# Threshold attention and gated MLP: first pair shaped in the score banks, and another order of the PSUM banks in the tail

## Chip, cores and metric

The kernel runs on one core of a Trainium2 chip. The metric is the device time of one execution in microseconds (us); the time of a version is the median over its runs.

## What is computed

Eight batches, eight heads, 576 positions, 64 channels a head. The attention keeps only the scores that lie within tau = 0.02 of the largest of their row; its output is the input of a gated MLP with 512 inputs and 1024 inner channels.

```python
scores = scale * np.matmul(q, k.transpose(0, 1, 3, 2))           # scale = 1/8
thresh = np.max(scores, axis=-1, keepdims=True) - tau
scores = np.where(scores >= thresh, scores, -1000000000.0)
attn = softmax(scores);  x = matmul(attn, v), heads side by side  # (8, 576, 512)
h = np.maximum(x @ w_in, 0.0);  u, v = h[..., :512], h[..., 512:]
v_n = (v - mean(v)) / sqrt(var(v) + 1e-6)
v_s = einsum('ts,bsd->btd', w_spatial, v_n) + b_spatial[None, :, None]
out = (u * v_s) @ w_out
```

## The kernel before

**Units of work.** Two heads form a pair; there are 32 pairs, four a batch. A pair has five chunks of query rows: four of 128 (c = 0 to 3), and a rest of 64 rows; the rests of two neighbouring pairs are joined into one chunk of 128 rows (c = 4), done with the odd pair. That makes 144 steps. The order is written out by hand: each engine does its instructions in program order, and only semaphore waits decide when.

**Before a pair's scores** q and k must be transposed, so that channels lie on partitions. `shape_qk` (L130) copies a pair's loaded q and k into transposable form on GpSimd (POOL); for the first pair `shape_first` (L142) does it on VectorE (DVE), ScalarE (ACT) and POOL at once. Then come three jobs on TensorE (PE): `qk_main(i, 0)` transposes the four blocks of q and ACT copies them, times 1/8, into `qkT` (L243, L248); `qk_main(i, 1)` does so for k (L243, L250); `qk_rem` transposes the one block that holds the last 64 rows of q and of k (L259), ACT copies it into `qkT` (L262), and from there the last 64 keys are copied into `kd`, a block-diagonal matrix of both heads, by two copies of 64x64 (L267): DVE for the first pair, POOL for all others. In the head of the program these three jobs of pair 0 stand alone, one after the other (L773), after 14 dummy transposes (L769) that keep PE busy.

**A step** (`step`, L558) first issues the scores on PE: one matmul a pair against `kd` for the 128 last keys of both heads (L529), and one a head for the first 512 keys (L534). Then come one or two other jobs on PE (transposes of the next pair, probabilities times values, MLP matmuls), the row maximum on DVE (L570), the exponentials on ACT (L593, or L587 and L589 for chunks 2 and 4), and the thresholding of the step before on DVE (L551), after which SyncE (SP) issues the transposing DMA of the probabilities, `pT` (L555; L546 for joined chunks, into `ptr`). Two steps or more later `pv` and `pv_rest` multiply by the values (L273, L278), and DVE divides by the row sums (L285, L287). The MLP of a batch runs 26 steps and more after the batch began, as jobs in the steps: `moe_v` (L402, L387, L390), `moe_u` (L444, L449), `moe_s` (L474, L479) and `moe_o` (L503).

**PSUM** has eight banks of 512 floats a partition. In the steps six belong to the pool `ps_s`: two score tiles `s` of three banks each, in turn. The other two are the pool `ps_f` (tiles `f`, one bank each, in turn), for every other job. A tile of a pool waits until all that read the tile before it in the same place are done[...].

**The tail** begins when step 143, the last, is issued. The pool `ps_s` is closed and its six banks become single-bank tiles `t` of a pool `ps_t`; each waits for the score tile that lay there. Jobs that are still due then follow each other without score steps (`run`, L806): `moe_v(6, 4)`, `pv_rest(15)`, `moe_u(6, 1)`, `moe_o(5, 0)`, `x_pe(30)` (L351), `moe_u(6, 2)`, `moe_o(5, 1)`, `moe_u(6, 3)`, `pv(31, 0)`, `moe_o(5, 2)`, `moe_u(6, 4)`, `moe_o(5, 3)`, `pv(31, 1)`, the `moe_s(6, ...)`, and then the last batch (`last_gmlp`, L618). `bank` (L220) chooses the place: its counter runs from the start of the program, and every fourth tile is an `f`, the others are `t`. In the profiled execution the first twelve places of the tail are, by the names in the trace, t t t f t t t f t t t f.

Of the kernel before, what the change touches and what calls it, by code (L numbers as in the profile page):

```python
# [8 lines left out]
F32 = mybir.dt.float32  # L9
# [8 lines left out]
def kernel(  # L18
# [17 lines left out]
    nc = tc.nc  # L36
    B, H, S, D = q.shape
    assert (B, H, S, D) == (8, 8, 576, 64)
    scale = 0.125
# [3 lines left out]
    P = 128  # L43
    const = ctx.enter_context(tc.tile_pool(name="const", bufs=1))
    qkn = ctx.enter_context(tc.tile_pool(name="qkn", bufs=2))
    qkT = ctx.enter_context(tc.tile_pool(name="qkT", bufs=2))
# [12 lines left out]
    ps_s = inner.enter_context(tc.tile_pool(name="ps_s", bufs=2, space=PSUM))  # L59

    identf = const.tile([P, P], F32, name="identf")
# [13 lines left out]
    kd_ring = [const.tile([P, P], F32, name=f"kd{i}") for i in range(2)]  # L75
# [25 lines left out]
    def load(i, n, w, eng=nc.sync):  # L101

        b, hp = divmod(i, HP)
        t = ld_ring[i // 2 % 2][w][:, 2 * (i % 2):2 * (i % 2) + 2 * n]
        src = (q, k, v)[w][b, 2 * hp:2 * hp + 2 * n]

        def main():
            eng.dma_start(
                out=t[:, :, 0:4, :],
                in_=src[:, 0:512, :].rearrange("h (p c) d -> p h (c d)", c=4))  # L110

        def rest():

            u = ld_ring[i // 2 % 2][(0, 0, 2)[w]][(slice(0, 64), slice(64, 128), slice(0, 64))[w]]
            eng.dma_start(out=u[:, 2 * (i % 2):2 * (i % 2) + 2 * n, 4, :],
                          in_=src[:, 512:576, :].rearrange("h p d -> p h d"))

        def rest_b():
            nc.sync.dma_start(
                out=vx_ring[i // 2 % 2][64:128],  # L120
                in_=src.rearrange("(j h) s d -> h s j d", h=2)[1, 512:576])
        return [main, rest] + ([rest_b] if w == 2 else [])
# [5 lines left out]
    nat = {}  # L128
# [39 lines left out]
    def load_w_in(f):  # L168
        nc.sync.dma_start(out=wsl[f % 3].rearrange("p c s -> p (c s)")[:, 0:1024],
                          in_=moe_w_in[f * P:(f + 1) * P, :])  # L170
# [46 lines left out]
    wide = []  # L217
    turn = [0]

    def bank(dtype=F32, n=512):  # L220
        turn[0] += 1
        if wide and turn[0] % 4:
            return wide[0].tile([P, n], dtype, name="t")
        return ps_f.tile([P, n], dtype, name="f")

    def bank16():

        return bank(BF16, 640)

    qks, pts, xns, xts = {}, {}, {}, {}  # L230
# [4 lines left out]
    def qk_main(i, which):  # L235
        hold = {}

        def mm():
            if which == 0:
                qks[i] = qkT.tile([P, 2, S], F32, name="qkT")  # L240
            t = hold["t"] = bank()
            for c in range(4):
                nc.tensor.transpose(out=t[:, c * P:(c + 1) * P], in_=nat[i][which][:, c, :],  # L243
                                    identity=identf)

        def ev():
            if which == 0:
                nc.scalar.mul(out=qks[i][:, 0, 0:512], in_=hold["t"], mul=scale)  # L248
            else:
                (nc.scalar.copy if i else nc.vector.tensor_copy)(out=qks[i][:, 1, 0:512],  # L250
                                                                 in_=hold["t"])
        return "act", mm, ev

    def qk_rem(i):
        hold = {}

        def mm():
            t = hold["t"] = bank()
            nc.tensor.transpose(out=t[:, 0:P], in_=nat[i][0][:, 4, :], identity=identf)  # L259

        def ev():
            nc.scalar.copy(out=qks[i][:, :, 512:576],  # L262
                           in_=hold["t"][:, 0:P].rearrange("p (w s) -> p w s", w=2))
            kd = kd_ring[i % 2]
            for lo in (0, 64):
                hs = slice(lo, lo + 64)
                (nc.gpsimd if i else nc.vector).tensor_copy(out=kd[hs, hs],  # L267
                                                            in_=qks[i][hs, 1, 512:576])
        return "act", mm, ev

    def weigh(t, at, pt, vt):

        nc.tensor.matmul(out=t[:, at:at + 130], lhsT=pt[:, 4, :],  # L273
                         rhs=vt[:, 4:6, :].rearrange("p b d -> p (b d)"),
                         start=True, stop=False)
        for h in range(2):
            for j in range(4):
                nc.tensor.matmul(out=t[:, at + 65 * h:at + 65 * h + 65], lhsT=pt[:, 5 * h + j, :],  # L278
                                 rhs=vt[:, 6 * h + j, :], start=False, stop=(h == 1 and j == 3))
# [454 lines left out]
    for b in range(B):  # L734
        n = dict.fromkeys("vuso", 0)
        for j, t in enumerate(ORDER):
            f = {"v": moe_v, "u": moe_u, "s": moe_s, "o": moe_o}[t]
# [14 lines left out]
    with tc.manual_schedule():  # L752
        for w in (0, 1):
            for f in load(0, 1, w, (nc.sync, nc.scalar)[w]):
                f()
        make_identity(nc, identf)
        clear()
        nc.vector.memset(ntau, -float(tau))
        nc.vector.memset(mhalf, -0.5)
        nc.scalar.activation(out=ctau, in_=ntau, func=ACT.Exp)  # L760
        nc.vector.tensor_copy(out=identb, in_=identf)
        for w in (0, 1):
            for f in load(1, 1, w):
                f()
        for f in load(0, 2, 2):
            f()
        for j in range(3):
            load_w_in(j)
        for _ in range(14):  # L769
            nc.tensor.transpose(out=ps_f.tile([P, 512], F32, name="f")[:, 0:P], in_=identf,  # L770
                                identity=identf)
        shape_first()
        for f in (qk_main(0, 0), qk_main(0, 1), qk_rem(0)):  # L773
            f[1]()
            f[2]()
        shape_qk(1)
        queue = []
        for g, (i, c) in enumerate(steps):
            if c == 2 and i + 2 < NPAIR:
                shape_qk(i + 2)  # L780
            if c == 0:
                shape_v(i)
            if c == 0 and i % 2 and i + 3 < NPAIR or g == 0:
                for w in range(3):
                    queue.extend(load(i + (3 if g else 2), 2, w))
            if g in chores:
                chores[g][0](chores[g][1])
            fs, small_ones = [], []
            if i + 1 < NPAIR and c < 3:
                fs.append(qk_rem(i + 1) if c == 1 else qk_main(i + 1, c // 2))  # L790
            if i and c == (2 if i % 2 else 3):
                fs.append(pv(i - 1, 0))
            if i > 1 and c == 4:
                fs.append(pv(i - 2, 1))
            if i % 2 and c == 3:
                fs.append(pv(i - 1, 1))
            if i % 2 and i > 1 and c == 1:
                small_ones = [pv_rest(i // 2 - 1)]
                fs += small_ones
            fs += [f(*a) for f, *a in jobs.get(g, [])]  # L800
            fs.sort(key=lambda f: (f[0] == "dve", f in small_ones))
            sends += queue[:1 if g > 3 else 2]
            del queue[:1 if g > 3 else 2]
            step(i, c, fs)

        def run(*fs):  # L806
            for f in fs:
                f[1]()
                f[2]()
                for f in sends:  # L810
                    f()
                sends.clear()
        while held:
            held.pop(0)()
        mask()
        inner.close()
        wide.append(ctx.enter_context(tc.tile_pool(name="ps_t", bufs=6, space=PSUM,
                                                  reuse_waits="tile")))
        for _, f in later:
            f()  # L820
        last = [f(b, j) for f, b, j in last]
        run(last[0], pv_rest(NPAIR // 2 - 1), *last[1:3], x_pe(NPAIR - 2), *last[3:6],
            pv(NPAIR - 1, 0), *last[6:], pv(NPAIR - 1, 1), moe_s(Z - 1, 0), moe_s(Z - 1, 1),
            x_pe(NPAIR - 1, True), *[moe_s(Z - 1, j) for j in range(2, 5)])
        rest = last_gmlp(Z)
        next(rest)
        run(moe_u(Z, 0), moe_u(Z, 1))
        next(rest)
        run(*[moe_u(Z, j) for j in range(2, 5)], *[moe_o(Z - 1, j) for j in range(4)])
        next(rest)  # L830
        next(rest, None)
# [35 lines left out]
```

## Time and profile before

| | us |
|---|---|
| median of 6 runs | 483.67 |
| lowest and highest run | 481.24, 485.29 |
| profiled execution, its own time | 482.22 |
| its span, first to last instruction | 480.4 |
| PE busy in the span | 449.0 (93%) |
| DVE busy | 416.7 (87%) |
| ACT busy | 381.8 (79%) |
| POOL busy | 226.6 (47%) |
| first score matmul starts | 8.52 |
| last step's row maximum, start and end | 438.03, 439.39 |
| last step's exponentials, start and end | 439.41, 440.79 |

In a view's line the first numbers are start and duration in us from the start of the span, then engine, source line, operation, output and inputs, with the number of instructions merged into the line; brackets hold the idle time before it and what ended it. PEld is the weight load of a matmul. The chain of waits goes back from the last instruction to what released each one. A table of stretches gives busy time and instruction count of each engine, then the granted clock of PE as a part of full speed (PEclk), the busy share of the 16 DMA engines and GB/s.

### The profile page before, as it was taken

To read this page: it belongs to the slowest core of one execution; us is meant where nothing else is said; L and a number is where in the kernel's file an instruction comes from. 1 tells how busy PE (TensorE), PEld (TensorE's weight loads), DVE (VectorE), ACT (ScalarE), POOL (GpSimd) and SP (SyncE) were. 2 spreads that over 40 slices of the span, in tenths; PEclk is the share of its full clock that TensorE was granted. 3 is DMA by queue.
4 is the path that set the end of the run, shared out by engine and by line. 5 is a ranking of instruction groups with operands and counts; after the bars stand their busy time and mean duration, and the time that the engine had idled before them with its cause. 6 is when DMAs were issued, how large, how long until landed. Compare 5 with 4: busy or idle time off the path is not lost.

```text
span 480.4 us, 9896 instructions
## 1 busy us (share of the span) xinstructions
PE 449.0 (93%) x3664; PEld 238.3 (50%) x3664; DVE 416.7 (87%) x563; ACT 381.8 (79%) x665; POOL 226.6 (47%) x403
## 2 busy tenths in 40 slices
PE   7788788889999999999999999999999999997995
PEld 4344444444554555554555545555554545444542
DVE  4899999989989997999889989899889988897573
ACT  2788787998879798788979898789978888896251
POOL 3462435784438543474417642475337733352021
PEclk8999999999999999999999999999999999999999
DMA  7799999979999799898979889997997999765423
GB/s 236 198 206 213 211 229 193 233 167 191 182 198 196 169 218 209 196 168 190 214 174 223 184 201 212 199 172 174 212 209 189 182 170 206 161 114 111 133 82 117
DMA packets 231120, 89.38 MB, mean 186 GB/s; under 512 B 200608, under 2 KB 225312, under 8 KB 231072
## 3 DMA queue, kind: packets, MB, share of 16 engines
q1 hardware_dynamic: 230416, 87.86, 85.8%
q8 instruction: 29, 0.48, 0.4%
q0 software_dynamic: 160, 0.52, 0.3%
q10 hardware_dynamic: 496, 0.36, 0.2%
q14 instruction: 19, 0.16, 0.1%
HBM read 33.31 MB, written 9.44 MB: 89 GB/s over the span
## 4 chain that ended last, share of the span: by engine, by line
PE 47%; DVE 22%; ACT 21%; issue 5%; DMA 3%; POOL 0%; SPq 0%; POOLq 0%; ACTq 0%; DVEq 0%
PE s L534 13%; DVE negm L570 10%; DVE p L551 8%; ACT e L593 5%; PE f L243 5%; PE f L503 4%; ACT e L587 4%; PE f L278 4%; PE s L529 4%; DMA pT<-p 3%; PE f L444 3%; ACT vrel L412 2%; ACT sq L426 2%; ACT p L589 2%; PE f L273 2%
## 5 line engine op out<-in xcount | busy, mean ns | idle before, releaser
L570 DVE TENSOR_REDUCE negm<-s 128x2 f32<-128x1152 f32 x144 | 194.8, 1353 | 27.5 <-PE s L534 27.0
L534 PE MATMUL s<-qkT 64*128 64x512 f32 (+1 forms) x640 | 162.9, 639 | 0.0
L551 DVE SCALAR_TENSOR_TENSOR p<-e,ctau 128x1152 bf16<-128x1152 f32 x96 | 138.7, 1445 | 1.4 <-ACT e L593 1.2
L593 ACT ACTIVATE e<-s,negm 128x576 f32<-128x576 f32 x192 | 131.8, 742 | 6.5 <-DVE negm L570 6.2
L587 ACT ACTIVATE e<-s,negm 128x576 f32<-128x576 f32 x96 | 65.9, 738 | 19.7 <-DVE negm L574 11.1
L529 PE MATMUL s<-kd,qkT 128*128 128x128 f32 (+1 forms) x320 | 64.7, 305 | 14.2 <-ACT e L593 9.6
L267 POOL COPY kd<-qkT 64x64 f32<-64x64 f32 x62 | 30.4, 491 | 93.9 <-ACT qkT L262 92.1
L529 PEld LDWEIGHTS s<-kd,qkT 128*128 128x128 f32 (+1 forms) x320 | 44.4, 180 | 33.8 <-ACT e L593 19.7
L534 PEld LDWEIGHTS s<-qkT 64*128 64x128 f32 (+1 forms) x640 | 42.1, 175 | 18.3 <-issue 3.0
L420 POOL TENSOR_SCALAR nmean<-sm 128x1 f32<-128x1 f32 (+1 forms) x35 | 15.2, 435 | 69.7 <-ACT vrel L412 64.4
L278 PEld LDWEIGHTS <-pT 128*128 128x128 bf16 x1024 | 41.8, 97 | 7.3 <-issue 4.8
L278 PE MATMUL f<-v,pT 128*128 128x65 bf16 x992 | 44.9, 194 | 0.0
L136 POOL COPY qn<-ql 128x640 f32<-128x640 f32 x31 | 34.8, 1122 | 21.1 <-DMA ql<-in_k_dram 16.2
L589 ACT ACTIVATE p<-e 128x1152 bf16<-128x1152 f32 x32 | 37.2, 1164 | 1.0
L250 ACT COPY qkT<-f 128x512 f32<-128x512 f32 x31 | 18.2, 587 | 16.8 <-PE f L243 16.8
L273 PE MATMUL f<-v,pT 128*128 128x130 bf16 x124 | 27.2, 220 | 3.7 <-ACT qkT L250 1.6
L432 POOL TENSOR_SCALAR vn<-vrel,rs,nm 128x512 bf16<-128x512 f32 (+1 forms) x34 | 28.5, 840 | 3.7
L474 PE MATMUL f<-wsT,vn 128*128 128x512 bf16 x120 | 29.8, 379 | 0.0
L402 PE MATMUL f<-w_in,xT 128*128 128x512 bf16 x112 | 28.9, 380 | 0.0
L444 PE MATMUL f<-xT,w_in 128*128 128x512 bf16 x108 | 27.9, 380 | 0.8 <-DVE xn L287 0.8
L287 DVE TENSOR_TENSOR xn<-f,r 128x256 bf16<-128x256 f32 x62 | 26.3, 425 | 2.1
L248 ACT ACTIVATE qkT<-f 128x512 f32<-128x512 f32 x32 | 18.8, 589 | 10.7 <-PE f L243 10.0
(163 smaller groups left out, 639.6 us busy)
## 6 DMA issues: line engine op xcount, KB each, us to landing
vl<-in_v_dram SPq DMA_DIRECT2D x16, 512.0 KB, 4.7
ql<-in_q_dram SPq DMA_DIRECT2D x15, 512.0 KB, 4.8
kl<-in_k_dram SPq DMA_DIRECT2D x15, 512.0 KB, 4.7
out_dram<-o SPq DMA_DIRECT2D x20, 256.0 KB, 3.2
uT<-in_moe_w_in_dram SPq DMA_DIRECT2D x3, 512.0 KB, 5.4
uT<-in_moe_w_spatial_dram SPq DMA_DIRECT2D x2, 576.0 KB, 4.5
vl<-in_v_dram SPq DMA_DIRECT2D x16, 64.0 KB, 4.4
pT<-p SPq DMA_TRANSPOSE x64, 5.6
```

The costliest lines, as they stand in the source:

```text
L136: nc.gpsimd.tensor_copy(out=t, in_=ld_ring[i // 2 % 2][w][:, 2 * (i % 2):2 * (i % 2) + 2].rearrange("p h c d -> p c h d"))
L267: (nc.gpsimd if i else nc.vector).tensor_copy(out=kd[hs, hs], in_=qks[i][hs, 1, 512:576])
L273: nc.tensor.matmul(out=t[:, at:at + 130], lhsT=pt[:, 4, :], rhs=vt[:, 4:6, :].rearrange("p b d -> p (b d)"), start=True, stop=False)
L278: nc.tensor.matmul(out=t[:, at + 65 * h:at + 65 * h + 65], lhsT=pt[:, 5 * h + j, :], rhs=vt[:, 6 * h + j, :], start=False, stop=(h == 1 an ...
L444: nc.tensor.matmul(out=t, lhsT=w_in[:, m, f * P:(f + 1) * P], rhs=xts[b][:, m, 0:512], start=(m == 0), stop=(m == 3))
L529: nc.tensor.matmul(out=view(s[rows], 512, [[448, 2], [1, 64]]), lhsT=qks[n][:, 0, m], rhs=kd_ring[n % 2], start=True, stop=True)
L534: nc.tensor.matmul(out=s[rows, 1024 * h:1024 * h + 512], lhsT=qks[n][hs, 0, m], rhs=qks[n][hs, 1, 0:512], start=True, stop=True)
L551: nc.vector.scalar_tensor_tensor(out=pt[:, c % 2, :], in0=ef, scalar=ctau, in1=ef, op0=ALU.is_ge, op1=ALU.mult)
L570: nc.vector.tensor_reduce(out=nm, in_=s, axis=AX.X, op=ALU.max, negate=True)
L587: nc.scalar.activation(out=e[:, h, :], in_=s[:, h, :], func=ACT.Prelu, bias=nm[:, h:h + 1], scale=by, alpha=1e30)
L589: nc.scalar.activation(out=pr_ring[i // 2 % 2] if c == 4 else p_ring[2 * (i % 2) + c // 2][:, c % 2], in_=e.rearrange("p h s -> p (h s)"), ...
L593: nc.scalar.activation(out=e[:, h, :], in_=s[:, h, :], func=ACT.Exp, bias=nm[:, h:h + 1])
```

## The change

Three things. Pair 0 gets a function of its own, `first`, in place of `qk_main(0, 0)`, `qk_main(0, 1)` and `qk_rem(0)`: nine transposes, five of q into one score tile and four of k into another, without a wait for banks between them; then ACT copies q, two DVE copies fill `kd` straight from PSUM, ACT and DVE copy one half of k each, and ACT copies the last block. `qk_main` and `qk_rem` lose their branches for pair 0; for the other pairs they are what they were. And `bank` counts from the start of the tail alone and gives in every eight tiles the places t f f t t t t t.

```diff
     def bank(dtype=F32, n=512):
-        turn[0] += 1
-        if wide and turn[0] % 4:
-            return wide[0].tile([P, n], dtype, name="t")
+        if wide:
+
+            turn[0] += 1
+            if turn[0] % 8 not in (2, 3):
+                return wide[0].tile([P, n], dtype, name="t")
         return ps_f.tile([P, n], dtype, name="f")
...
+    def first():
+
+        qkt = qks[0] = qkT.tile([P, 2, S], F32, name="qkT")
+        ts = [ps_s.tile([P, 1536], F32, name="s") for _ in range(2)]
+        for t, w, c, at in ([(ts[0], 0, c, c * P) for c in range(5)]
+                            + [(ts[1], 1, c, c * P) for c in range(4)]):
+            nc.tensor.transpose(out=t[:, at:at + P], in_=nat[0][w][:, c, :], identity=identf)
+        nc.scalar.mul(out=qkt[:, 0, 0:512], in_=ts[0][:, 0:512], mul=scale)
+        for lo in (0, 64):
+            hs = slice(lo, lo + 64)
+            nc.vector.tensor_copy(out=kd_ring[0][hs, hs], in_=ts[0][hs, 576:640])
+        nc.scalar.copy(out=qkt[:, 1, 0:256], in_=ts[1][:, 0:256])
+        nc.vector.tensor_copy(out=qkt[:, 1, 256:512], in_=ts[1][:, 256:512])
+        nc.scalar.copy(out=qkt[:, :, 512:576],
+                       in_=ts[0][:, 512:640].rearrange("p (w s) -> p w s", w=2))
...
         shape_first()
-        for f in (qk_main(0, 0), qk_main(0, 1), qk_rem(0)):
-            f[1]()
-            f[2]()
+        first()
         shape_qk(1)
```

## The prediction

> **What bounds the kernel now.** I first read the page's busy shares and chain: no engine is full, and the end is set by PE, DVE and ACT in turn.
>
> ```profile
> PE 449.0 (93%) x3664; PEld 238.3 (50%) x3664; DVE 416.7 (87%) x563; ACT 381.8 (79%) x665; POOL 226.6 (47%) x403
> PE 47%; DVE 22%; ACT 21%; issue 5%; DMA 3%; POOL 0%; SPq 0%; POOLq 0%; ACTq 0%; DVEq 0%
> ```
>
> So the 144 steps drive themselves: a step starts when the last ends, and loads are issued from the steps. Time gained before the first step should arrive at the last, if nothing tied to the clock on the wall lies between. The change touches only the two ends, so I read those closely. The chain of waits, 6 to 11 us:
>
> ```profile
> 6.21 0.61 ACT qkT L248
> ...
> 6.95 0.32 PE f L259
> ...
> 7.29 0.28 ACT qkT L262
> ...
> 7.59 0.19 DVE kd L267
> ...
> 7.79 0.69 DVE kd L267
> ...
> 8.52 0.49 PE s L529 x2
> 9.01 1.57 PE s L534 x4
> ```
>
> From the q copy to the first scores each step waits for the one before: L259 for the bank that q leaves, then a copy, then `kd` from that copy. Then the table of stretches, cut where PE's clock changes:
>
> ```profile
> 5.98:9.39 3.41, 1.80 (x11) 1.13 (x11) 1.55 (x3) 0.86 (x2) 1.28 (x2) 1.00 0.95 246
> 9.39:12.81 3.42, 3.42 (x12) 1.75 (x10) 1.36 (x1) 1.15 (x3) 0.90 (x2) 0.51 0.96 369
> 16.22:19.63 3.41, 1.87 (x10) 0.80 (x10) 3.38 (x5) 2.31 (x5) 0.83 (x1) 1.00 0.29 72
> ```
>
> After 3.41 us in which PE was busy for only 1.80, the next 3.42 run at half clock, with PE busy throughout. Last, the timeline where the tail starts:
>
> ```profile
> 438.03 1.35 DVE L570 TENSOR_REDUCE negm<-s 128x2 f32<-128x1152 f32 x1
> 438.49 0.58 ACT L459 ACTIVATE uT<-f 128x512 bf16<-128x512 f32 x1
> 439.41 1.37 ACT L593 ACTIVATE e<-s,negm 128x576 f32<-128x576 f32 x2 [0.34 <-DVE negm L570]
> 439.49 0.10 PEld L273 LDWEIGHTS <-ptr 128*128 128x128 bf16 x1 [0.83 <-issue]
> 439.50 0.42 DVE L287 TENSOR_TENSOR xn<-f,r 128x256 bf16<-128x256 f32 x1
> 440.84 0.22 PE L273 MATMUL t<-v,ptr 128*128 128x130 bf16 x1 [1.69 <-ACT e L593]
> 442.31 1.03 PE L503 MATMUL f<-w_o,gT 128*128 128x512 bf16 x4
> ```
>
> The first `t` (`moe_v(6, 4)`, 438.09) waits for nothing late, but the second, `pv_rest`, starts only when the last step's exponentials end. So it lies where the last score tile was. Meanwhile the `f` banks fall free at 439.07 (L459 ends) and 439.92 (L287 ends), unused until 442.31. From 440.84 to 473.32 the chain is PE alone, without a gap: what PE gains here, the end gains.
>
> [...] here one 53% busy was followed by the dip, while 1.87 us (55%) from 16.22 was not. [...] in `x_pe(31)` both read halves of one bank, and DVE starts as ACT ends:
>
> ```profile
> 452.06 0.37 ACT L360 COPY xT<-f 128x256 bf16<-128x256 bf16 x1 [3.52 <-PE f L354]
> 452.46 0.29 DVE L361 COPY xT<-f 128x256 bf16<-128x256 bf16 x1
> ```
>
> [...]
>
> **The head, step by step.** Transposes: q's four finish as before (6.19). The fifth needs POOL's L149, which ended at 5.80; it costs one slot. Four k transposes' loads take 0.59 us, so 0.15 a slot: the fifth is done about 6.35, k's four at 6.61 + 0.15 = 6.76, plus 0.04 for the wait. ACT: q 6.21 to 6.82 as before; half of k, 0.37 (L360's row is bf16 but has 256 columns; the 64x256 float copy L695 took 0.37 too): to 7.19; last block, 0.27 as L262: to 7.46. DVE: two `kd` copies from PSUM of 64 columns. No such row exists: between 0.17 (L285, 4 columns from PSUM) and 0.42 (L491, 256 columns)[...]. I take 0.2 each, 6.37 to 6.8, ends 6.7 and 7.2; either way ahead of ACT. DVE's half of k shares its bank with ACT's, so it follows at 7.22 and takes 0.42: to 7.64. The first score tile takes the place of the first transposes' tile, so L529 waits for all its readers, the last being ACT at 7.46; L534 wants DVE's half of k at 7.68, but L529 before it lasts to 7.99. **First score 7.5 for 8.52: 1.0 us.** Bounds: 0.6 (slow `kd` copies and ACT's last copy queued behind them) to 1.2.
>
> The clock. With PE at work 5.98 to 6.8 and from 7.5 on, the window to 9.39 is 2.7 us busy of 3.41, well over the 1.80. Even if the dip came all the same, at the same place, more of PE's work lies before it: L534 at full clock takes 1.1 instead of 1.57 (7.99 to 9.1), the transposes L243 0.6 instead of 1.04 (qn was ready at 8.42), to 9.7; L529 and L534 of the second step at half clock 1.92 as now, to 11.6 instead of 13.54. The row maximum of step 1 ends at 13.0, thresholding of step 0 (1.42, free to start as its exponentials end about 12.0) at 14.4, and the third row maximum starts at 14.4, where the chain has it at 16.38. **So 2.0 us by then, 1.0 of it the clock's.** Without a dip it is about 2.5. [...]
>
> What could stop it on the way: POOL's copy of pair 2 waits for its load until 18.80, wherever the steps are; PE wants it at 23.37, now 21.4, and it ends at 19.7. The first transposing DMA (issued 19.19) would come at 17.2; the loads ahead of it leave the DMA engines idle from 17.2 to past 20, so it has room. Every later DMA is issued from steps. SP and POOL get no added instruction; two copies stay on DVE.
>
> **The tail.** `pv_rest` goes to the first `f`: start 439.13 (439.07 and a wait) for 440.84, takes 0.61; `moe_u(6, 1)` to the second: 439.98 (behind it PE's queue waits, as now), 0.86, to 440.84; `moe_o(5, 0)` to the second `t`, free at 440.84: where it now starts at 442.31. **1.47 us.** Behind it all banks are free or reused after eight tiles, as now. One guard: the last `pT`, issued at 442.3 and 4.6 us on its way, lands at 446.9; `pv(31, 1)` is due at 448.80 − 1.47 = 447.3, its weights 0.2 earlier. Margin 0.2, so I take **1.4**. ACT can't follow at first (440.68 on), but the banks give it four tiles of slack.
>
> ```profile
> L555 SPq DMA_TRANSPOSE pT<-p x2: 2683/2708/2733, 438.2 to 442.3; - x2
> ...
> DMA to landing us min/median/max: 4.6/4.6/4.6
> ```
>
> Bank copies of pairs 1 to 31 are untouched: 0.
>
> **Sum.** 2.0 + 1.4 = 3.4 on the profiled execution's 482.22 (span 480.4 and 1.8 around it): 478.8. That execution is 1.45 below the median of the runs, 483.67; off the median it is 480.3, or 481.3 for runs without a dip. I say 480.5.
>
> **Rivals.** *Only the tail counts* (14%): the head's gain is lost among steps that wait for transposing DMAs (3% of the chain). For: DMA engines are over 90% busy in many slices. Against: they are idle before the first transpose. 483.67 − 1.4 = 482.3. *Only the head counts* (13%): the last `pT` lands later, as the median of 5.6 us over all would have it: 447.9, 0.8 behind its weights' due time, and what hangs on it keeps PE waiting; then some 0.6 of the tail is left at best, none if more is late: 481.1 to 481.7. *Slower* (6%): the shift moves `pT` behind 512 KB loads more often. The chain holds two such waits, 6.47 and 7.18 us, against 4.7 for the shortest at the start: some 2.3 each. From the second more on the gain is gone; with three more, 480.5 + 6.9 = 487.4. Against: all are issued from the same queue in the same order. *It doesn't do what it says* (3%): were the `f` banks not free first, or the tiles' waits wider, 483.7.
>
> **Numbers.** The forecast case has 64%, its own range 479.0 to 481.9. A measurement tells 0.5% (2.4 us) from no change at best, so faster means under 481.25: four fifths of the forecast case and part of the second rival. The range 478.8 to 483.0 leaves out the slower case, part of "nothing happens", and gains over the bound.
>
> **What would show it.** First L529 near 7.5; no `f` tile in the head but the dummies; DVE's half of k right after ACT's; PEclk at 1.00 through 9.4 to 12.8, or L534 of step 0 at 1.1; the first `pT` issued about 17; in the tail `pv_rest` on an `f`, 0.4 to 0.5 us after `moe_v(6, 4)`'s last matmul instead of 2, and `moe_o(5, 0)` right as the last exponentials end, then PE without gaps. I'm wrong if PE stalls at `pv(31, 1)`, or the last exponentials end less than 1 us earlier than 440.79.

## Result, and the profile after

The changed kernel takes 479.78 us (median of 29 runs, 478.32 to 482.92), the kernel before 482.75 beside it (64 runs, 480.13 to 487.45): a ratio of 0.9946, interval 0.9932 to 0.9959. By that ratio it is 2.6 us less; the two medians by themselves are 3.0 apart. The profiled executions are 478.95 and 482.22 us, 3.3 apart. In the fences of after, line numbers are higher by 16 from `pv` on (L529, L534, L570 and L551 of before are L545, L550, L586 and L567); `first` is L277 to L284.

The page's busy shares and the chain's shares by engine:

```profile
PE 447.4 (94%) x3664; PEld 237.8 (50%) x3664; DVE 416.5 (87%) x563; ACT 381.6 (80%) x666; POOL 225.7 (47%) x403
PE 46%; DVE 24%; ACT 21%; issue 6%; DMA 2%; POOL 1%; POOLq 0%; ACTq 0%; DVEq 0%
```

The work is the same and so is its mix; only the two ends moved. The chain of waits of after, from the transposes to the third row maximum:

```profile
5.24 1.08 PE s L277 x5
6.34 0.61 ACT qkT L278
6.97 0.22 DVE kd L281
7.20 0.24 DVE kd L281
7.46 0.28 ACT qkT L284
7.78 0.49 PE s L545 x2
...
13.93 1.28 DVE negm L586
```

The first score starts at 7.78 (8.52 before) and the third row maximum at 13.93 (16.38). The steps between are handed on one by one: q's copy starts only when the fifth transpose, in the next bank of the same tile, has ended; the `kd` copies, which read that other bank, start only when q's copy has ended. The timeline shows DVE idle until ACT's copy of q is done:

```profile
6.97 0.46 DVE L281 COPY kd<-s 64x64 f32<-64x64 f32 x2 [2.42 <-ACT qkT L278]
6.99 0.37 ACT L282 COPY qkT<-s 128x256 f32<-128x256 f32 x1
```

So these readers of one score tile take turns, though they read different banks of it. (DVE's half of k starts at 7.46, when DVE is done with `kd`; whether it also waited for ACT can't be seen here.) The table of stretches at the same times as before (columns: stretch, its length, busy us of PE, PEld, DVE, ACT, POOL, then PE's clock, the DMA share, GB/s):

```profile
5.98:9.39 3.41, 2.58 (x13) 1.47 (x12) 0.89 (x4) 1.23 (x3) 1.27 (x2) 1.00 0.83 233
9.39:12.81 3.42, 2.68 (x15) 1.49 (x17) 2.91 (x3) 2.30 (x5) 1.30 (x4) 1.00 0.85 302
16.22:19.63 3.41, 1.65 (x13) 0.59 (x14) 3.01 (x3) 3.12 (x4) 0.22 (x1) 1.00 1.01 222
```

PE has 2.58 us of work where it had 1.80, and the stretch behind it, at 0.51 before, runs at 1.00. Last the tail's timeline:

```profile
437.26 0.22 PE L289 MATMUL f<-v,ptr 128*128 128x130 bf16 x1
437.56 1.37 ACT L609 ACTIVATE e<-s,negm 128x576 f32<-128x576 f32 x2 [0.34 <-DVE negm L586]
438.13 1.04 PE L460 MATMUL f<-xT,w_in 128*128 128x512 bf16 x4
439.00 1.03 PE L519 MATMUL t<-w_o,gT 128*128 128x512 bf16 x4
```

`pv_rest` now stands ahead of the last exponentials, on an `f`; `moe_u(6, 1)` follows on the second, and `moe_o(5, 0)` starts at 439.00 as they end (437.56 + 1.37 = 438.93). It was at 442.31, so 3.31 us have arrived here. The last transposing DMA pair is issued 1.86 us earlier (436.32 for 438.18), so **1.86 us of the 3.31 came down from the head and 1.45 were made in the tail**. The `pT` is in time: `pv(31, 1)` starts at 445.49 without a wait.

```profile
L571 SPq DMA_TRANSPOSE pT<-p x2: 2674/2688/2702, 436.3 to 440.4; - x2
DMA to landing us min/median/max: 4.6/4.6/4.6
```

### The profile page after: what moved, and what is told of

Its sections match the earlier page's. It is cut to its first block, busy times and chain, and to the rows that moved or that the text cites. A ratio compares the mean times of both kernels' runs of the same rounds, so it can differ in the third digit from the quotient of the medians.

```text
span 477.1 us, 9894 instructions
## 1 busy us (share of the span) xinstructions
PE 447.4 (94%) x3664; PEld 237.8 (50%) x3664; DVE 416.5 (87%) x563; ACT 381.6 (80%) x666; POOL 225.7 (47%) x403
## 4 chain that ended last, share of the span: by engine, by line
PE 46%; DVE 24%; ACT 21%; issue 6%; DMA 2%; POOL 1%; POOLq 0%; ACTq 0%; DVEq 0%
PE s L550 13%; DVE negm L586 11%; DVE p L567 8%; ACT e L603 5%; ACT e L609 5%; PE f L245 4%; PE f L294 4%; PE f L519 4%; PE s L545 4%; PE f L460 3%; ACT vrel L428 2%; ACT sq L442 2%; ACT p L605 2%; PE f L490 2%; PE f L289 2%
## 5 line engine op out<-in xcount | busy, mean ns | idle before, releaser
L586 DVE TENSOR_REDUCE negm<-s 128x2 f32<-128x1152 f32 x144 | 194.8, 1353 | 26.2 <-PE s L550 25.5
L550 PE MATMUL s<-qkT 64*128 64x512 f32 (+1 forms) x640 | 161.9, 636 | 0.0
L567 DVE SCALAR_TENSOR_TENSOR p<-e,ctau 128x1152 bf16<-128x1152 f32 x96 | 139.6, 1455 | 1.3 <-ACT e L609 0.9
L545 PE MATMUL s<-kd,qkT 128*128 128x128 f32 (+1 forms) x320 | 64.3, 304 | 12.9 <-ACT e L609 8.6
L545 PEld LDWEIGHTS s<-kd,qkT 128*128 128x128 f32 (+1 forms) x320 | 44.2, 179 | 32.2 <-ACT e L609 18.7
L550 PEld LDWEIGHTS s<-qkT 64*128 64x128 f32 (+1 forms) x640 | 41.9, 174 | 18.2 <-issue 2.7
L436 POOL TENSOR_SCALAR nmean<-sm 128x1 f32<-128x1 f32 (+1 forms) x35 | 15.6, 446 | 68.0 <-ACT vrel L428 62.7
L448 POOL TENSOR_SCALAR vn<-vrel,rs,nm 128x512 bf16<-128x512 f32 (+1 forms) x34 | 29.5, 868 | 3.7
L490 PE MATMUL f<-wsT,vn 128*128 128x512 bf16 x125 | 31.1, 379 | 0.0
L428 ACT ACTIVATE vrel<-f 128x512 f32<-128x512 f32 (+1 forms) x34 | 20.1, 592 | 7.4 <-PE f L418 5.0
```

What stands on the lines that cost most here:

```text
L490: nc.tensor.matmul(out=t, lhsT=vn[:, c, f * P:(f + 1) * P], rhs=wsT[:, c, 0:512], start=(c == 0), stop=(c == 4))
L545: nc.tensor.matmul(out=view(s[rows], 512, [[448, 2], [1, 64]]), lhsT=qks[n][:, 0, m], rhs=kd_ring[n % 2], start=True, stop=True)
L550: nc.tensor.matmul(out=s[rows, 1024 * h:1024 * h + 512], lhsT=qks[n][hs, 0, m], rhs=qks[n][hs, 1, 0:512], start=True, stop=True)
L567: nc.vector.scalar_tensor_tensor(out=pt[:, c % 2, :], in0=ef, scalar=ctau, in1=ef, op0=ALU.is_ge, op1=ALU.mult)
L586: nc.vector.tensor_reduce(out=nm, in_=s, axis=AX.X, op=ALU.max, negate=True)
```

## Experiments

Granted clock: below, a run "at full clock" is one whose mean granted clock is 0.997 or more. One half-speed stretch of 3.41 us takes 3.41 × 0.5 / 480 = 0.0036 off that mean, so such a run has none while PE has work. (In the traces the last 0 to 2.9 us, behind PE's last work, are at half clock as well; the 2.9 us of after alone take its mean to 0.997, so a run at 0.996 can be either.) Of the 143 runs of before that stand beside the experiments 49 are at full clock, median 481.05, the others have 483.27; of after it is 16 of 29, 479.38 and 480.82. The clock is not the whole spread: single runs of before at full clock take 485 us.

Dummy transposes, where an experiment adds them, write to tiles that nothing reads; no experiment leaves out any of the computation.

### One part at a time: e1 the head, e2 the tail

e1 is after with the old order of banks, e2 is before with the new one:

```diff
 # e1, against after
-    turn = [0]
+    turn = [3]
...
-        if wide:
-            turn[0] += 1
-            if turn[0] % 8 not in (2, 3):
-                return wide[0].tile([P, n], dtype, name="t")
+        turn[0] += 1
+        if wide and turn[0] % 4:
+            return wide[0].tile([P, n], dtype, name="t")
```

> The new head (pair 0 in the score tiles) with the old places of the tail (t t t f). My theory (the head gives 0.7 us of path, and about 0.5 more in the median because some runs of the kernel before lose clock there; the tail gives 1.45): 1.2 us less than before, ratio 0.9975; first score at 7.8, the tail's second tile still waits for the last exponentials, 1.7 us of idle PE. Rival 'only the tail counts' (the head's gain is lost among the steps): ratio 1.000. Rival 'the head is all': ratio 0.9946.

> The old head with the new places of the tail (t f f t t t t t). My theory: 1.45 us less than before, ratio 0.9970, second tile 0.4 us after the first one's last matmul, PE without gaps behind it. Rival 'only the tail counts': 2.6 us, ratio 0.9946. Rival 'the head is all': ratio 1.000. The head's clock shows a half-speed stretch of 3.4 us in this profile or not[...].

Measured: e1 481.15 (22 runs), ratio 0.9979 (0.9962 to 0.9996); e2 481.05 (22 runs), 0.9962 (0.9944 to 0.9980). Their product is 0.9941, after has 0.9946: the parts add up, and each of the rivals "only the tail" (by e1's interval, which just ends under 1) and "only the head" falls. Head 1.0 us, tail 1.8, with intervals of about 0.8 either way.

At full clock e1 has 480.94 (12 runs) and e2 479.99 (8): the tail is then worth 1.1 (e2 against before) to 1.6 (after against e1), the head 0.1 (e1 against before) to 0.6 (after against e2). So a large part of the head's worth seems to lie in the clock: 64 to 66% of the runs of before and e2 are below full clock, 45% of those of after and e1. The pieces of the new head (shared tiles without waits, `kd` straight from PSUM, k copied by two engines) were not run one by one. The profiled run of e2 has the old head's dip (8.79 to 12.20, behind a stretch with 1.80 us of PE's work), and a second one later:

```profile
15.62:19.03 3.41, 1.67 (x9) 0.63 (x8) 3.38 (x5) 2.30 (x5) 0.00 (x0) 1.00 0.66 163
19.03:22.44 3.41, 3.41 (x16) 1.20 (x16) 1.86 (x2) 2.48 (x3) 2.38 (x6) 0.50 0.75 140
```

### e3: only the clock, in the kernel before

```diff
 # e3, against before
             f[2]()
+        for _ in range(2):
+            fill = ps_s.tile([P, 1536], F32, name="s")
+            for c in range(4):
+                nc.tensor.transpose(out=fill[:, c * P:(c + 1) * P], in_=identf, identity=identf)
         shape_qk(1)
```

> The kernel before, with eight dummy transposes on PE between the last transpose of pair 0 and the first scores, where PE sat idle from 7.25 to 8.52; they write into two score tiles that nobody reads. The path to the first scores stays as it was (8.5). Theory that PE's lost clock is part of the head's cost: no half-speed stretch behind 9.4, third row maximum at 15.0 to 15.4 instead of 16.4 where the stretch was; over the runs 0.4 to 0.7 us less than before, ratio 0.9986 to 0.9992. Rival (the clock is an accident that no filling changes, or its loss is taken back later): ratio 1.000 or, if the dummies delay the first scores, up to 1.0005.

Measured: 483.23 (14 runs), 1.0006 (0.9984 to 1.0027), no gain. In its profile the early dip is gone (third row maximum 15.28 for 16.38), but the first score comes at 8.99 for 8.52, and two stretches from 20.2 to 27.0 run at half clock. Only 1 of 14 runs is at full clock. So it doesn't give the clock's worth by itself: it moved the low spot and made no run better. Inconclusive on the size, but it showed that the dip has more than one place.

### e4: the head without the shared tiles

The last block and the second half of k go to two `f` tiles, so that DVE and ACT read different tiles:

```diff
 # e4, against after
-        for t, w, c, at in ([(ts[0], 0, c, c * P) for c in range(5)]
-                            + [(ts[1], 1, c, c * P) for c in range(4)]):
+        r, k1 = [ps_f.tile([P, 512], F32, name="f") for _ in range(2)]
+        for t, w, c, at in ([(ts[0], 0, c, c * P) for c in range(4)] + [(r, 0, 4, 0)]
+                            + [(ts[1], 1, c, c * P) for c in range(2)]
+                            + [(k1, 1, c, c * P - 256) for c in range(2, 4)]):
```

> The changed kernel, with pair 0's last block and second half of k transposed into the two f banks, so that four tiles have one or two readers each. Theory (the changed head lost 0.3 us because readers of one score tile were made to wait for each other: q's copy for the fifth transpose, kd for q's copy, the last block's copy for kd): kd copies start at 6.4 instead of 6.97, first score at 6.9 instead of 7.8, and the third row maximum 0.5 us earlier than the 13.9 of the changed kernel; ratio to before 0.9930 to 0.9940 against 0.9946 for the change. Rival (copies wait for something else, or POOL's copy for pair 1 at 8.0 to 9.3 holds the second step): third row maximum within 0.1 us of 13.9, ratio 0.9946.

Measured: 479.30 (6 runs), 0.9924 (0.9893 to 0.9954). Timeline of e4:

```profile
5.97 0.60 ACT L280 ACTIVATE qkT<-s 128x512 f32<-128x512 f32 x1 [0.76 <-PE s L279]
6.10 0.46 DVE L283 COPY kd<-f 64x64 f32<-64x64 f32 x2 [1.57 <-PE f L279]
6.70 0.46 PE L547 MATMUL s<-kd,qkT 128*128 128x128 f32 x2 [0.20 <-ACT qkT L280]
...
21.02 0.66 PE L245 MATMUL f<-identf,qn 128*128 128x128 f32 x4 [0.90 <-POOL qn L136]
```

With tiles apart DVE copies beside ACT: q's copy starts 0.37 us earlier than in after, `kd` 0.87 (6.10 for 6.97), and the first score is at 6.70, 1.08 ahead of after. So the wait by tile is what held them, and the theory was right, with a larger size than expected. But the time is that of after within the interval (at full clock, as all six runs are, 479.29 against 479.38). PE now waits at 21.02 for pair 2. Its load is tied to the clock on the wall: it lands at about 19 us however early the steps are (in e4's chain one piece of 8.52 us, from 10.67 to 19.19). And POOL's copy of it, from 19.48, takes 1.48 us for the usual 0.72, beside a thresholding on DVE (18.98 to 20.39). By an estimate from these figures (0.90 less 0.76), PE would have waited some 0.1 us without that. More of the lead is lost later, as the section on the prediction tells.

### e5, e6, e8: pair 2's load ahead of the MLP's weights

```diff
 # e5, against after; e6 the same against e4, e8 against before
-    chores = {3: (load_bias, 0), 7: (shape_bias, 0)}
+    chores = {2: (lambda _: [load_w_in(j) for j in range(3)], 0), 3: (load_bias, 0),
+              7: (shape_bias, 0)}
...
-        for j in range(3):
-            load_w_in(j)
         for _ in range(14):
```

> The changed kernel with the three loads of w_in (512 KB each) issued behind the loads of q and k of pairs 2 and 3 instead of ahead of them. Theory (part of the head's gain is lost because pair 2's load lands at 19.2 us whatever the head does, so that POOL's copies of it fall on DVE's thresholding, 1.83 and 2.22 us for 1.41): the load lands at 14 to 15, thresholding near 20 us takes 1.4 again, 0.4 to 0.8 us less than the change, ratio to before 0.9928 to 0.9938. Rival (what is lost between 17 and 31 us is lost to the transposing DMAs): ratio 0.9946, thresholding as before.

> The head with four tiles apart and the same order of loads. Theory: PE no longer waits 0.9 us for POOL's copy of pair 2 at 21.0, and the 0.9 us that this head gains by the third row maximum reach the end: 0.9 to 1.4 us less than the change, ratio to before 0.9917 to 0.9928. Rival (the steps behind are bound by the transposing DMAs, which take back what comes early): not better than the head apart alone, 0.9924 to 0.9935, the gain over the kernel before falling from 3 us at the first transposing DMA to 2 at the second.

> The kernel before with the order of loads of the fifth experiment. Theory: in the kernel before the copy of pair 2 lies in a gap and nobody waits for its load, so nothing is to be had: ratio 0.998 to 1.001. Rival (the order of loads is a gain of its own): the same 0.4 to 0.8 us as there, ratio 0.9983 to 0.9992 in the middle.

Measured: e5 481.22 (22 runs), 0.9956 (0.9935 to 0.9977); e6 478.70 (9), 0.9932 (0.9896 to 0.9967); e8 483.43 (22), 1.0010 (0.9987 to 1.0034). My theory was that the late load lets POOL's copies fall beside DVE's thresholding, and that an earlier load frees it. It fell for e5: POOL's copies start at 14.66 for 19.41, but the two long thresholdings are there all the same, 4.8 us earlier:

```profile
15.31 1.83 DVE L567 SCALAR_TENSOR_TENSOR p<-e,ctau 128x1152 bf16<-128x1152 f32 x1
19.85 2.22 DVE L567 SCALAR_TENSOR_TENSOR p<-e,ctau 128x1152 bf16<-128x1152 f32 x1
```

and behind them two stretches at half clock, the second although PE was busy for 2.97 of 3.41 us in the first:

```profile
16.02:19.43 3.41, 1.46 (x12) 0.41 (x12) 3.41 (x3) 2.94 (x5) 3.29 (x7) 1.00 0.60 175
19.43:22.84 3.41, 2.97 (x7) 1.25 (x8) 2.73 (x4) 2.92 (x4) 1.44 (x2) 0.50 0.97 203
22.84:26.26 3.42, 3.42 (x11) 1.69 (x11) 1.30 (x2) 1.86 (x3) 0.00 (x0) 0.50 0.97 212
```

8 of 22 runs of e5, 4 of 22 of e8 and 4 of 9 of e6 are at full clock, rather fewer than of after and before, though so few runs don't make that sure. In the runs at full clock alone the new order is ahead each time: by 0.4 us in e5 (479.01 against after's 479.38), 0.5 in e8 (480.59 against 481.05) and 0.85 in e6 (478.45 against e4's 479.29). So e8's rival, a gain of the order itself, is not out; the ratios of all runs show none. e6's ratio lies in its rival's range, with an interval that takes in the theory's as well.

### e7, e9: filling the low spots

e7 adds four dummy transposes to each of the first seven steps, e9 only to the two steps around the low spot that after still has (15.4 to 19.8 us):

```diff
 # e9, against after; e7: if i == 0 or i == 1 and c in (4, 0, 1)
+        if (i, c) in ((0, 3), (1, 4)):
+            fill = ps_f.tile([P, 512], F32, name="f")
+            for n in range(4):
+                nc.tensor.transpose(out=fill[:, n * P:(n + 1) * P], in_=identf, identity=identf)
         nm = small.tile([P, 2], F32, name="negm")
```

> The changed kernel with four dummy transposes on PE in each of the first seven steps, behind the step's other PE work, written into an f bank that nobody reads. Theory (runs lose up to 2 us when one or two half-speed stretches fall into the first 26 us, where PE is busy for only 55 to 80 per cent; the granted clock of the whole run shows it): mean granted clock 0.998 or more in all runs, none under 0.996 where the change had 12 of 29, median 0.3 to 0.7 us less than the change, ratio to before 0.9930 to 0.9940. Rival (the clock dips are set by something else, or the dummies hold up the scores): clock spread as before, ratio 0.9946 or worse by up to 0.6 us each 0.15 us of delay in a step, 0.9955.

> The changed kernel with four dummy transposes on PE behind the scores of steps 3 and 4 only, where PE waits 1.25 and 1.1 us for exponentials anyway (15.6 to 16.9 and 18.3 to 19.4). In the five traces with half-speed stretches each stretch followed a window of 3.41 us with PE busy for 1.46 to 1.80, none one with 1.87 or more; in the changed kernel the only such windows start between 15.4 and 16.4. Theory (that is what the changed kernel's runs with a low granted clock lose): no profile with a half-speed stretch, nearly all runs at a mean granted clock of 0.997 or more, median at that of the change's own runs of full clock, 479.4, or 0.3 to 0.6 us less than the change. Rival (dummies on PE cost time wherever they are, as the seven steps of them did): 480.2 or more.

Measured: e7 482.58 (22 runs), 0.9986 (0.9967 to 1.0006): the theory fell. 14 of 22 runs are at full clock, hardly more than the 16 of 29 of after, and there it takes 481.79, 2.4 more than after. In its profile PE is busy without a break from 9.39 to 16.22: there it has no slack, and the dummies stand in its queue. e9 478.89 (11 runs), 0.9934 (0.9908 to 0.9961), all 11 at full clock, as the theory had it. Its stretch there:

```profile
16.22:19.63 3.41, 2.30 (x18) 1.09 (x18) 3.01 (x3) 3.05 (x4) 0.20 (x1) 1.00 0.95 187
```

2.30 us where after had 1.65. With 16 of 29 without the dummies, 11 of 11 here and 25 of 26 in e10 and e11 below, most runs of after below full clock must come from that spot. Two things don't fit so simple an account: e7 fills these two steps as well, and its profile has no 3.41 us with less than 1.86 us of PE's work before the tail, yet 8 of its runs are below full clock; and e4, with nothing filled and two spots down to 1.46 and 1.55 in its profile, has all six at full clock. In time e9 is not clear of after: the intervals overlap.

### e10, e11: the versions put together

e11 is e4 with e9's dummies, e10 is that with the loads in e6's order.

> The head with four tiles apart, the loads of w_in last, and the same dummies in steps 3 and 4. Theory: 478.2 to 478.7, every run at 0.997 or more, ratio to before 0.9905 to 0.9920. Rival (the dummies cost): 479 or more.

> The head with four tiles apart, the loads in their old order, and the same dummies. Theory: 0.3 to 0.5 us less than the change with the dummies, since PE waits for pair 2's load here: 478.8 to 479.2; ratio 0.9915 to 0.9930. Rival: as good as with the loads reordered, 478.5.

Measured, on one chip with e9: e10 478.46 (9 runs, 477.99 to 479.69), 0.9919 (0.9893 to 0.9946); e11 479.25 (17 runs), 0.9930 (0.9908 to 0.9951). e10 came out as expected, e11 at the edge of its range. e10 has the lowest median of all, 1.3 us under after's; its interval overlaps those of e9 and e11, and of after, so that it beats them isn't shown. e10 and e11 differ in the order of the loads alone, and nearly all their runs are at full clock (9 of 9, 16 of 17). In e10's profile one thresholding of the first 40 us is long (1.88), in e11's three are (1.83, 2.23, and 1.94 at 39.16); these two executions are 1.3 us apart, the medians 0.8.

## Why the prediction was right, and where a size was off

The forecast was 480.5 us; 479.78 was measured, with the mechanism of the forecast case: both ends gain. Off the profiled execution it said 3.4 and got 3.27. That this is so near is in part luck: the head's 2.0 came out as 1.86 because a gain larger than forecast by the third row maximum (2.45) met a loss on the way that the sum put at nothing. The base moved too: 483.67 was the median of six runs, 64 have 482.75, so off the median the forecast was 3.2 us less, against the 2.6 measured. And "481.3 for runs without a dip" took the smaller gain off a median made mostly of runs with a dip; at full clock before takes 481.05 and after 479.38.

**The tail: right.** 1.47 was worked out and 1.4 taken; the trace has 1.45, and e2 and e1 give 1.1 to 1.6 at full clock. No `pT` was late, so the rival "only the head" had nothing to stand on, and `pv_rest` is on an `f`, so "it doesn't do what it says" fell as well.

**The head path: the term "1.0 us" was too large.** At the first score 0.74 was gained, inside the bounds of 0.6 to 1.2. The step that failed is that of the two `kd` copies: "I take 0.2 each, 6.37 to 6.8, ends 6.7 and 7.2; either way ahead of ACT". Their size, an estimate between rows of 0.17 and 0.42, was right (0.22 and 0.24), their start was not: 6.97, behind ACT's q copy, since the waits go by the score tile and not by the bank. The fifth transpose held q's copy for the same reason: it starts at 6.34, not at 6.21 as before. e4 showed it by taking the sharing away: `kd` at 6.10, q's copy at 5.97.

**"Time gained before the first step should arrive at the last": not all of it.** By the first `pT` 2.45 us had been gained (16.74 for 19.19), at the end 1.86. Between lie two thresholdings of after; the kernel before has one of 1.93 there, and all others of the first 36 us, in both, take 1.41 to 1.42:

```profile
20.07 1.83 DVE L567 SCALAR_TENSOR_TENSOR p<-e,ctau 128x1152 bf16<-128x1152 f32 x1
24.61 2.22 DVE L567 SCALAR_TENSOR_TENSOR p<-e,ctau 128x1152 bf16<-128x1152 f32 x1
```

```profile
22.36 1.93 DVE L551 SCALAR_TENSOR_TENSOR p<-e,ctau 128x1152 bf16<-128x1152 f32 x1
```

Above 1.41 that is 0.42 + 0.81 = 1.23 against 0.52: 0.71 more. The lead of the row maxima over before falls in the same steps, from 2.45 us at the fifth step to 1.74 at the twelfth, and is 1.86 at the last. The trace has POOL's copies and casts from 19.41 to 27 around both of after, and two casts (22.37 to 24.39) beside the one of before. Over the whole spans 10 of the 96 thresholdings of before and 11 of the 96 of after take 1.60 to 2.30 us, each beside a copy or cast of POOL; of the others, which take 1.50 at most, 50 of 86 and 48 of 85 have work of POOL beside them as well. And of the two like `kd` copies in the head of before (L267) the second, beside a POOL copy (7.70 to 8.42), takes 0.69 us for 0.19. So the long ones are found beside POOL's copies; what in the engines holds them up isn't shown. Those copies wait for a load tied to the clock on the wall (19.41, 18.80 before), so steps that come earlier fall on them differently.

The price can be read by itself at later places. In e1 a thresholding at 39 us (L565 there) runs beside POOL's copy of k for a later pair:

```profile
38.97 1.83 DVE L565 SCALAR_TENSOR_TENSOR p<-e,ctau 128x1152 bf16<-128x1152 f32 x1
38.98 0.61 POOL L136 COPY kn<-kl 128x512 f32<-128x512 f32 x1
```

It takes 0.42 too long, and the short scaling of `negm` before it 0.54 for the usual 0.17, beside POOL's copy of q. Together that is 0.79, and at this step e1's lead over before falls by 0.79, for good: 1.97 to 1.18. The same sum fits in e2 (0.58 too long, 0.59 lost), e4 (0.61 and 0.61 at 38 us, 0.47 and 0.47 at 62.7), e5 (0.65 and 0.65 at 65.7) and e11 (0.99 and 1.00); after, e6, e9 and e10 have no long thresholding between 26 and 90 us and lose nothing at 39. So what DVE loses beside POOL's copies reaches the end, and 1.08 us of e4's lead went there. For after's own loss the size fits, but there the scalings of `negm` are 0.4 longer than in before too and can't all have reached the end, so that the long thresholdings alone took the 0.71 isn't shown. e5 doesn't help, as its excess only moved.

**The clock: right in kind.** The third row maximum "starts at 14.4" came at 13.93, as there was no dip at all, the case given as "about 2.5". In all runs the parts are, by medians: at full clock after gains 1.7 on before (481.05 − 479.38), below it 2.45 (483.27 − 480.82), which with the share of before (34% and 66%) is 2.2; the change of share, from 66% to 45% of runs below, times the 1.4 that such a run of after costs, is 0.3. Together 2.5; the ratio gives 2.6. By this estimate the clock's part is what exceeds 1.7, some 0.8, for the 1.0 of the forecast. Of the head in runs at full clock, where the forecast's 2.0 less the clock's 1.0 leaves 1.0, 0.1 to 0.6 was left.

What I missed is the second low spot, 15.4 to 19.8: I had read 1.87 us from 16.22 as safe, in one window position. Stretches that begin at 15.6 to 16.0 or 17.6 to 18.8 hold 1.46 to 1.8 in before. It is where most of the 45% of runs of after that are still below full clock come from, and e9 closes it.

**The rivals.** *Only the tail* fell with e1 (0.9979, interval under 1), *only the head* with e2. *Slower*: the lead of the `pT` issues falls to between 0.3 and 0.7 around 72 to 98 us, once to nothing at 101, and comes back to 1.8. The steps don't follow: their row maxima there start 1.42 to 1.77 us earlier than before. So these DMAs were issued later, while the steps' own lead fell by no more than 0.3 us.

## What to carry to other kernels

In this program copies by two engines out of one PSUM tile took turns even where they read different banks (`kd` at 6.97 for 6.10 with tiles apart), so give each engine's part a tile of its own if it should start early; and read which stage is next before paying for it, since a load tied to the clock on the wall (here pair 2's), and copies on POOL that then run beside DVE's work, may take all of it (1.08 us in e4). A gain ahead of the first step can be worth more in clock than in time on the path (here, by estimate, 0.8 us against 0.1 to 0.6): slide a window of 3.41 us, the length of the half-speed stretches here, over PE's busy time, in every position, and look at all spots with 1.80 us or less, the most that was followed by half clock here, as places to try, not as a sure sign. Fill those spots with dummy work only where PE has slack: with two steps filled all 11 runs were at full clock (what that gains in time lies within the intervals), and with seven filled runs at full clock took 2.4 us more.

## What the runs showed of the hardware that was not expected

Half-speed stretches here follow windows of 3.41 us in which PE was busy for 1.46 to 1.80 us (before, e2 twice, e3, e5, e8: six of six, those behind PE's last work apart), and at full clock none follows a window of the same traces' grid (steps of 3.41 us from where the clock changes) with 1.87 or more. The reverse does not hold: in the tail, windows of the grid with 1.68 us (e1, from 437.72) and 1.75 us (e8, from 437.12) stayed without one (the mean clocks of these two profiles, 1.0 and 0.994, leave no room for it). So PE's busy time as a trace gives it is no sharp limit. Going back up took more: in e3 and e5 a half-speed window with 2.81 and 2.97 us of work was followed by another, and all six returns to full clock in these traces came behind a window busy throughout (3.41).

A load of pair 2, issued behind the MLP's weights, took 8.5 us from issue to landing (10.67 to 19.19 in e4's chain); moved ahead of them, its POOL copy started at 14.66 for 19.41.
